# Token-major queries, softmax divided out on chip, and both signs of a head pair turned into one 128-row operand

## Chip, cores, metric

One core of a Trainium2 chip. The metric is the device time of one execution in microseconds (us). Numbers are of runs with a mean granted TensorE clock of 0.996 to 1.0, unless a text says otherwise.

## The reference

A linear-attention branch and a GELU branch over the same 2048 tokens, mixed by a gate. bf16 throughout; 16 heads of 28; the hidden layer has 1792 features.

```python
q, k, v = heads(x @ wqkv)                                  # x: [2048, 448]
pq, pk  = q @ w_phi[h], k @ w_phi[h]
phi_q   = concat(softmax(pq), softmax(-pq))                # two signs, 56 features a head
phi_k   = concat(softmax(pk), softmax(-pk))
kv, z   = phi_k^T @ v, sum over tokens of phi_k
a = (phi_q @ kv) / (phi_q . z + 1e-6), heads merged, @ wo
b = gelu(x @ w1 + b1) @ w2 + b2
g = sigmoid((x * gate_w).sum(-1))
return g * a + (1 - g) * b
```

## The kernel before

The kernel folds `w_phi` into the query and key weights (`Wpq`, `Wpk`), so that one product of x gives the scores. TensorE works through stages: start-up and first key units; query scores `pq` alternating with the last keys and values; the hidden layer `hp`, with the key-value sums `acc` in its midst; then the output stage, in which each tile of 128 tokens has numerators `nm`, the second dense product `y` over w2, and the attention output with `wo`. NPR = 8 is the number of head pairs, PW = 56, KW = 60, HP = 64, NG = 4, NK = 7, NJ = 14.

Keys are token-major: 128 tokens by all 448 features, normalised in place. Queries are feature-major and stay unnormalised; their softmax sums are carried as extra columns and divided out per tile by VectorE.

```python
def k_norm(u):                                   # keys: divide the softmax sums out
    ...
    nc.vector.reduce_sum(out=sums[:], in_=ph, axis=AX.X)
    nc.vector.reciprocal(out=rec[:], in_=sums[:])
    ...                                          # product with rec on GpSimd (unit 7: half on VectorE)

def q_pair(g, h):                                # queries: feature-major, 512 tokens wide
    pq = four("pq")
    for k in range(NK):
        for i in range(2):
            nc.tensor.matmul(pq[:, i, :], lhsT=w_half(Wpq, WqS, i, k)[:, g * P:(g + 1) * P],
                             rhs=x_half(i, k, h), ...)
    nc.scalar.activation(out=EqP[:, g, dst], in_=src, func=ACT.Exp)
    nc.scalar.activation(out=EqN[:, g, dst], in_=src, func=ACT.Exp, scale=-1.0)

def k_two(r):                                    # keys of the second half: 448 wide
    ...
            nc.tensor.matmul(pk[:, i, 0:D], lhsT=x_half(i, k, 1)[:, r * P:(r + 1) * P],
                             rhs=w_half(Wpk, WkS, i, k), ...)

def num_tile(t):
    for g in range(NG):
        for s, E in ((0, EqP), (1, EqN)):        # 8 matmuls of 120 columns
            nc.tensor.matmul(nm[s][:, g * 2 * KW:(g + 1) * 2 * KW], lhsT=E[:, g, tok],
                             rhs=KVbd[:, g, s, :], start=True, stop=True)
    ...                                          # 12 VectorE operations in all, see the diff
    nc.sync.dma_start_transpose(oT[:, :, tok], o_tok[:, t % 4, :])
```

Half of x and half of each weight are wanted on the other 64 rows, so that two 64-row matmuls can run side by side. `xS` and `WqS` are those half-swapped copies, made by transfers; `WvS` and `WkS` are made by GpSimd.

```python
swap_on_pool(WvS, WvG)                           # GpSimd copies
...
nc.gpsimd.tensor_copy(out=WkS[0:HP, 0:3, :], in_=Wpk[HP:P, 0:3, :])
nc.gpsimd.tensor_copy(out=WkS[HP:P, 0:3, :], in_=Wpk[0:HP, 0:3, :])
swap_x(0, "even")                                # transfers issued by SyncE, in this order
swap_w(WqS, Wpq)
swap_x(0, "odd")
load_x(2)
load_x(3)
swap_x(1)                                        # xS of the second half
...
for n in range(2 * NJ):                          # hidden layer, 28 units
    m_unit(n // NJ, n % NJ)
    if n == 4:
        ...                                      # key-value sums
        gates()                                  # three small VectorE operations for the gate
```

The softmax here doesn't subtract the row's maximum and nothing guards it: scores larger than these inputs give would overflow.

Of the kernel before, what the change touches and what calls it, by code (L numbers as in the profile page):

```python
# [7 lines left out]
ALU = mybir.AluOpType  # L8
ACT = mybir.ActivationFunctionType
# [3 lines left out]
S = 2048  # L13
D = 448
H = 16
DH = 28
# [19 lines left out]
def kernel(  # L36
# [42 lines left out]
    EqP = consts.tile([P, NG, S], BF16, name="EqP")  # L79
    EqN = consts.tile([P, NG, S], BF16, name="EqN")  # L80
    oT = consts.tile([P, NC4, S], BF16, name="oT")
    o_tok = consts.tile([P, 4, 512], BF16, name="o_tok")
    KVbd = consts.tile([P, NG, 2, 2 * KW], BF16, name="KVbd")
# [18 lines left out]
    Wpq = attn.tile([P, NC4, NG * P], BF16, name="Wpq")  # L102
    WqS = attn.tile([P, NC4, NG * P], BF16, name="WqS")
# [4 lines left out]
    bd = w2_sb[:, 2:6, :].rearrange("p c (h d) -> p c h d", h=H)  # L108

# [12 lines left out]
    x0 = oT[:, 0, 0:4 * D].rearrange("p (t d) -> p t d", t=4)  # L122
# [42 lines left out]
    nc.gpsimd.memset(Wpq[:].rearrange("p c (x w) -> p (c x) w", w=HP)[:, :, PW:HP], 0.0)  # L165
# [11 lines left out]
    nc.gpsimd.memset(KVbd[:], 0.0)  # L177
    for g in range(NG):
        nc.gpsimd.tensor_copy(
            out=KVbd[:, g].rearrange("p s (i w) -> p s i w", i=2)[:, :, :, KW - 2:KW],  # L180
            in_=m4[:, None, :, :].to_broadcast([P, 2, 2, 2]))
# [82 lines left out]
    def wq_at(rows, c):  # L264
        return (Wpq[rows, c, :].rearrange("p i (x w) -> p i x w", w=HP)[:, :, :, 0:PW]
                if isinstance(c, slice)
                else Wpq[rows, c, :].rearrange("p (x w) -> p x w", w=HP)[:, :, 0:PW])

    def x_half(i, k, h):
        rows = slice(i * HP, (i + 1) * HP)  # L270
        b = 2 * h + i
        if k == NK - 1:
            return xS[rows, 3, h, :] if i == 0 else xT[rows, 3, b * 512:(b + 1) * 512]
        if k % 2 == i:
            return xT[rows, k // 2, b * 512:(b + 1) * 512]
        return xS[rows, k // 2, h, :]

    def k_exp(u, pk):
        tt = slice(2 * u, 2 * u + 2)
        src = pk[:, :, 0:D].rearrange("p i (x w) -> p i x w", w=PW)  # L280
        nc.scalar.activation(out=phik[:, tt, :, 0, 0:PW], in_=src, func=ACT.Exp)  # L281
        nc.scalar.activation(out=phik[:, tt, :, 1, 0:PW], in_=src, func=ACT.Exp, scale=-1.0)  # L282

    def k_norm(u):
        tt = slice(2 * u, 2 * u + 2)
        sums = work.tile([P, 32, 2], F32, name="sums", bufs=3)
        ph = phik[:, tt].rearrange("p t x s w -> p (t x s) w")[:, :, 0:PW]
        ph = ph.rearrange("p y (h d) -> p y h d", d=DH)
        nc.vector.reduce_sum(out=sums[:], in_=ph, axis=AX.X)  # L289
        rec = work.tile([P, 32, 2], F32, name="rec", bufs=3)  # L290
        nc.vector.reciprocal(out=rec[:], in_=sums[:])  # L291
        parts = [(nc.gpsimd, 0, 32)] if u < 7 else [(nc.vector, 0, 16), (nc.gpsimd, 16, 32)]
        for eng, lo, hi in parts:
            eng.tensor_tensor(out=ph[:, lo:hi], in0=ph[:, lo:hi],  # L294
                              in1=rec[:, lo:hi, :, None].to_broadcast([P, hi - lo, 2, DH]),
                              op=ALU.mult)

# [14 lines left out]
    def w_half(W, W_S, i, k):  # L312
        rows = slice(i * HP, (i + 1) * HP)
        if k == NK - 1:
            return W_S[rows, 3, :] if i == 0 else W[rows, 3, :]
        return W[rows, k // 2, :] if k % 2 == i else W_S[rows, k // 2, :]
# [17 lines left out]
    def q_pair(g, h):  # L334
        pq = four("pq")
        for k in range(NK):
            for i in range(2):
                nc.tensor.matmul(pq[:, i, :],  # L338
                                 lhsT=w_half(Wpq, WqS, i, k)[:, g * P:(g + 1) * P],
                                 rhs=x_half(i, k, h), start=(k == 0), stop=(k == NK - 1))  # L340
        dst = slice(h * 1024, (h + 1) * 1024)
        src = pq[:].rearrange("p a b -> p (a b)")
        nc.scalar.activation(out=EqP[:, g, dst], in_=src, func=ACT.Exp)  # L343
        nc.scalar.activation(out=EqN[:, g, dst], in_=src, func=ACT.Exp, scale=-1.0)  # L344
# [9 lines left out]
    def kv_out(acc):  # L354
        src = acc[:, 0, 0:NPR * (PW + 2)].rearrange("p (g i w) -> p g i w", g=NG, i=2)
        for s in range(2):
            for i in range(2):
                rows = slice(s * HP, s * HP + PW)
                nc.vector.tensor_tensor(
                    out=KVbd[i * HP:i * HP + PW, :, s, i * KW:i * KW + PW + 2],  # L360
                    in0=src[rows, :, i, :],
                    in1=mask[rows, None, :].to_broadcast([PW, NG, PW + 2]), op=ALU.mult)
# [46 lines left out]
    x1o = oT[0:HP, 1, 0:512]  # L409
    swap_on_pool(WvS, WvG)  # L410
    x0o = oT[0:HP, 1, 512:768]
# [24 lines left out]
    nc.sync.dma_start(w2_sb[:], B_w2.rearrange("(j p) n -> p j n", p=P))  # L436
# [3 lines left out]
    for g in range(NG):  # L440
        q_pair(g, 0)
    k_norm(3)
    for r in range(4):
        k_two(r)
        v_two(r)
        k_norm(4 + r)
        q_pair(r, 1)
# [14 lines left out]
    def m_unit(h, j):  # L462
        hp = wide("hp") if h == 0 and j == 2 else pair("hp")
        for k in range(NK):
            for i in range(2):
                nc.tensor.matmul(hp[:, i, :],  # L466
                                 lhsT=w1_sb[i * HP:(i + 1) * HP, k, j * P:(j + 1) * P],
                                 rhs=x_half(i, k, h), start=(k == 0), stop=(k == NK - 1))
        if gel[h] is None:
            gel[h] = hold.tile([P, NJ, S // 2], BF16, name="gel1", tag="phik_gel")  # L470
        nc.scalar.activation(out=gel[h][:, j, :],  # L471
                             in_=hp[:].rearrange("p a b -> p (a b)"),
                             func=ACT.Gelu_apprx_tanh, bias=b1T[:, j:j + 1])

    def num_tile(t):
        tok = slice(t * P, (t + 1) * P)
        nm_ps = ps2.tile([P, 2, 512], F32, name="nm", tag="nm", bufs=2)
        nm = [nm_ps[:, 0, :], nm_ps[:, 1, :]]
        for g in range(NG):
            for s, E in ((0, EqP), (1, EqN)):  # L480
                nc.tensor.matmul(nm[s][:, g * 2 * KW:(g + 1) * 2 * KW], lhsT=E[:, g, tok],  # L481
                                 rhs=KVbd[:, g, s, :], start=True, stop=True)
        nmv = [n_[:, 0:NPR * KW].rearrange("p (x w) -> p x w", x=NPR) for n_ in nm]
        st = work.tile([P, 2, NPR, 4], F32, name="st", bufs=3)
        for s in range(2):
            nc.vector.tensor_copy(out=st[:, s], in_=nmv[s][:, :, PW:KW])  # L486
        u = work.tile([P, 2, NPR, 2], F32, name="u", bufs=3)
        nc.vector.scalar_tensor_tensor(out=u[:], in0=st[:, :, :, 2:4], scalar=5e-7,
                                       in1=st[:, :, :, 0:2], op0=ALU.mult, op1=ALU.add)
        for s in range(2):  # L490
            nc.vector.tensor_tensor(out=u[:, s], in0=u[:, s], in1=st[:, 1 - s, :, 2:4],
                                    op=ALU.mult)
        den = work.tile([P, NPR, 2], F32, name="den", bufs=3)
        nc.vector.tensor_tensor(out=den[:], in0=u[:, 0], in1=u[:, 1], op=ALU.add)
        nc.vector.reciprocal(out=den[:], in_=den[:])
        al = work.tile([P, 2, NPR, 2], F32, name="al", bufs=3)
        tmp = work.tile([P, 2, D], BF16, name="tmp", bufs=2)
        for s in range(2):
            nc.vector.scalar_tensor_tensor(out=al[:, s], in0=den[:], scalar=eL[:, t:t + 1],
                                           in1=st[:, 1 - s, :, 2:4], op0=ALU.mult, op1=ALU.mult)  # L500
        for s in range(2):
            nc.vector.tensor_tensor(  # L502
                out=tmp[:, s, :].rearrange("p (x h d) -> p x h d", x=NPR, h=2),
                in0=nmv[s][:, :, 0:PW].rearrange("p x (h d) -> p x h d", h=2),
                in1=al[:, s, :, :, None].to_broadcast([P, NPR, 2, DH]), op=ALU.mult)
        nc.vector.tensor_tensor(out=o_tok[:, t % 4, 0:D], in0=tmp[:, 0, :], in1=tmp[:, 1, :],
                                op=ALU.add)
        nc.sync.dma_start_transpose(oT[:, :, tok], o_tok[:, t % 4, :])

    for n in range(2 * NJ):  # L510
        m_unit(n // NJ, n % NJ)
        if n == 4:
            acc = wide("acc")
            for u in range(8):
                kv_sum(acc, u)
            kv_out(acc)
            gates()
# [68 lines left out]
```

## Time and profile before

| | before |
|---|---|
| time, median of 3 runs | 155.48 us (155.42 to 156.28) |
| span of the profiled run | 153.5 us |
| first query matmul | 19.72 us |
| first matmul on `xS`, in the first key group of the second half | 25.77 us |
| first hidden-layer matmul | 42.44 us |
| first numerator | 88.69 us |
| last matmul ends | 150.16 us |

The stage limits in this table come from TensorE's timeline. The busy shares and the chain of waits are shown inside the prediction. The timeline of TensorE at the start of the second half's keys (start, duration, engine, line, what, output and inputs, shape, count):

```profile
25.76 0.35 PE L330 MATMUL pk<-Wpk,xT 64*128 64x448 bf16 x1
25.77 0.54 PE L330 MATMUL pk<-WkS,xS 64*128 64x448 bf16 x2
```

The matmul on `xT` and its partner on `xS` start 0.01 us apart: nothing is waited for. That distance is the measure of a wait for `xS`. The window of the hidden layer (window, then busy time and count of TensorE, its weight loads, VectorE, ScalarE and GpSimd, then granted clock, DMA share and GB/s):

```profile
42.40:88.70 46.30, 46.30 (x523) 22.61 (x519) 5.66 (x10) 33.11 (x32) 4.20 (x2) 1.00 0.09 29
```

TensorE is busy for all of the 46.3 us, VectorE and GpSimd for some 5 us each. This is the room into which the change puts its new work.

### The profile page before, as it was taken

The numbers are of one execution on the slowest core, as the hardware profiler recorded it, in microseconds if no ns is written. First come the engines' busy times: TensorE is split into PE (matmuls) and PEld (weight loads), VectorE is DVE, ScalarE is ACT, GpSimd is POOL, SyncE is SP. The second block draws the span as 40 slices with busy tenths as digits, with TensorE's granted clock in tenths as the row PEclk, the third lists the DMA queues.
The fourth block names the chain that finished last, engine by engine and source line by source line (L and its number), as shares of the span: only waits on it lengthen the run. The fifth ranks groups of instructions, "written<-read, shape, count | busy, mean of one in ns | idle before, by whom it ended". The sixth has DMA issues, their size and how long they took to land.

```text
span 153.5 us, 3192 instructions
## 1 busy us (share of the span) xinstructions
PE 148.4 (97%) x1302; PEld 78.1 (51%) x1302; DVE 83.1 (54%) x244; ACT 77.2 (50%) x93; POOL 40.0 (26%) x43
## 2 busy tenths in 40 slices
PE   7899999999999999999999999999999999999991
PEld 2464444444444944444444455555556555555560
DVE  3442899699890050000000069999977999977100
ACT  2665989998989347777676730111311111111121
POOL 7999497979873000000000000000000000000000
PEclk9999999999999999999999999999999999999999
DMA  4997999999990000000000001133332124235401
GB/s 153 212 228 154 205 193 213 219 218 216 251 343 12 4 0 4 0 0 4 0 0 0 4 0 34 34 63 77 91 94 64 41 70 92 77 83 38 124 30 30
DMA packets 27922, 14.11 MB, mean 92 GB/s; under 512 B 19842, under 2 KB 27780, under 8 KB 27908
## 3 DMA queue, kind: packets, MB, share of 16 engines
q1 hardware_dynamic: 26692, 13.25, 39.6%
q10 hardware_dynamic: 1152, 0.65, 1.5%
q8 instruction: 10, 0.16, 0.4%
q14 instruction: 4, 0.03, 0.1%
q0 software_dynamic: 64, 0.01, 0.0%
HBM read 6.11 MB, written 1.84 MB: 52 GB/s over the span
## 4 chain that ended last, share of the span: by engine, by line
PE 91%; DMA 3%; SPq 2%; issue 0%; DVE 0%; ACT 0%; ACTq 0%
PE y L525 28%; PE hp L466 28%; PE y L531 8%; PE pq L338 8%; PE nm L481 4%; PE v_ps L322 3%; PE pk L330 3%; DMA WqT<-in_A_wqkv_dram 3%; PE pk L223 3%; PE acc L349 2%; SPq L138 2%; PE v_ps L223 2%; PE w_ps L250 1%; PE pk L226 1%; SPq L126 1%; PE v_ps L226 0%
## 5 line engine op out<-in xcount | busy, mean ns | idle before, releaser
L525 PE MATMUL y<-w_sb,gel 128*128 128x448 bf16 (+2 forms) x238 | 45.2, 342 | 0.0
L466 PE MATMUL hp<-xT,w_sb 64*128 64x512 bf16 x196 | 42.6, 376 | 0.0
L466 PE MATMUL hp<-xS,w_sb 64*128 64x512 bf16 x196 | 42.6, 376 | 0.0
L471 ACT ACTIVATE gel<-hp,b1T 128x1024 bf16<-128x1024 f32 x28 | 30.8, 1110 | 13.0 <-PE hp L466 13.0
L534 ACT ACTIVATE res<-y,ungate 128x448 bf16<-128x448 f32 (+2 forms) x17 | 10.4, 611 | 50.3 <-PE y L531 50.2
L525 PEld LDWEIGHTS <-gel 128*128 128x128 bf16 x238 | 22.6, 98 | 19.6
L466 PEld LDWEIGHTS <-w_sb 64*128 64x128 bf16 x392 | 19.0, 94 | 23.0
L294 POOL TENSOR_TENSOR phik<-phik,rec 128x1792 bf16<-128x1792 bf16 (+1 forms) x8 | 24.9, 3127 | 6.1 <-DVE rec L291 6.1
L486 DVE COPY st<-nm 128x32 f32<-128x32 f32 x32 | 4.5, 184 | 35.5 <-PE nm L481 35.5
L502 DVE TENSOR_TENSOR tmp<-nm,al 128x448 bf16<-128x448 f32 x32 | 18.4, 617 | 0.0
L289 DVE TENSOR_REDUCE sums<-phik 128x64 f32<-128x1792 bf16 x8 | 16.0, 2000 | 4.0 <-ACT phik L282 4.0
L531 PE MATMUL y<-wo_sb,oT 128*128 128x448 bf16 (+2 forms) x68 | 14.7, 341 | 0.0
L338 PE MATMUL pq<-xT,Wpq 64*128 64x512 bf16 x56 | 12.9, 376 | 0.0
L338 PE MATMUL pq<-xS,WqS 64*128 64x512 bf16 x56 | 12.9, 376 | 0.0
L343 ACT ACTIVATE EqP<-pq 128x1024 bf16<-128x1024 f32 x8 | 8.4, 1051 | 2.2 <-PE pq L338 2.2
L197 DVE CAST vaug<-v_ps 128x896 bf16<-128x896 f32 x7 | 7.5, 1081 | 2.7 <-PE v_ps L209 1.7
L281 ACT ACTIVATE phik<-pk 128x896 bf16<-128x896 f32 x8 | 7.7, 961 | 1.8 <-PE pk L228 1.8
L344 ACT ACTIVATE EqN<-pq 128x1024 bf16<-128x1024 f32 x8 | 8.4, 1055 | 0.0
L481 PE MATMUL nm<-KVbd,EqP 128*128 128x120 bf16 x64 | 8.3, 216 | 0.0
L481 PE MATMUL nm<-KVbd,EqN 128*128 128x120 bf16 x64 | 8.3, 216 | 0.0
L282 ACT ACTIVATE phik<-pk 128x896 bf16<-128x896 f32 x8 | 7.8, 972 | 0.0
L531 PEld LDWEIGHTS <-oT 128*128 128x128 bf16 x68 | 6.0, 98 | 3.5
(105 smaller groups left out, 159.8 us busy)
## 6 DMA issues: line engine op xcount, KB each, us to landing
w_sb<-in_B_w_dram SPq DMA_DIRECT2D x4, 784.0 KB, 11.6
out_dram<-res SPq DMA_DIRECT2D x15, 112.0 KB, 1.9
w_sb<-in_B_w_dram SPq DMA_DIRECT2D x1, 1568.0 KB, 16.9
xS<-xT SPq DMA_DIRECT2D x2, 256.0 KB
oT<-in_A_x_dram ACTq DMA_DIRECT2D x1, 448.0 KB, 3.1
xS<-xT SPq DMA_DIRECT2D x2, 192.0 KB, 3.6
wo_sb<-in_A_wo_dram SPq DMA_DIRECT2D x1, 336.0 KB
WqS<-Wpq SPq DMA_DIRECT2D x1, 256.0 KB, 3.2
```

Of the source, the lines that this page charges most:

```text
L289: nc.vector.reduce_sum(out=sums[:], in_=ph, axis=AX.X)
L294: eng.tensor_tensor(out=ph[:, lo:hi], in0=ph[:, lo:hi], in1=rec[:, lo:hi, :, None].to_broadcast([P, hi - lo, 2, DH]), op=ALU.mult)
L338: nc.tensor.matmul(pq[:, i, :], lhsT=w_half(Wpq, WqS, i, k)[:, g * P:(g + 1) * P], rhs=x_half(i, k, h), start=(k == 0), stop=(k == NK - 1))
L343: nc.scalar.activation(out=EqP[:, g, dst], in_=src, func=ACT.Exp)
L344: nc.scalar.activation(out=EqN[:, g, dst], in_=src, func=ACT.Exp, scale=-1.0)
L466: nc.tensor.matmul(hp[:, i, :], lhsT=w1_sb[i * HP:(i + 1) * HP, k, j * P:(j + 1) * P], rhs=x_half(i, k, h), start=(k == 0), stop=(k == NK ...
L471: nc.scalar.activation(out=gel[h][:, j, :], in_=hp[:].rearrange("p a b -> p (a b)"), func=ACT.Gelu_apprx_tanh, bias=b1T[:, j:j + 1])
L481: nc.tensor.matmul(nm[s][:, g * 2 * KW:(g + 1) * 2 * KW], lhsT=E[:, g, tok], rhs=KVbd[:, g, s, :], start=True, stop=True)
L502: nc.vector.tensor_tensor(out=tmp[:, s, :].rearrange("p (x h d) -> p x h d", x=NPR, h=2), in0=nmv[s][:, :, 0:PW].rearrange("p x (h d) -> p ...
L525: nc.tensor.matmul(y, lhsT=gel[t // 8][:, j, (t % 8) * P:(t % 8 + 1) * P], rhs=w2_sb[:, j, cols], start=(j == 0), stop=False)
L531: nc.tensor.matmul(y, lhsT=oT[:, c, tok], rhs=wo_sb[:, c, cols], start=False, stop=(c == NC4 - 1))
L534: nc.scalar.activation(out=res[:, cols], in_=y, func=ACT.Copy, scale=ungate[:, t:t + 1])
```

## The change

The intent is to give the queries the form that the keys have already: token-major scores, 448 wide, softmax sums divided out once. The normalised units are then turned by DMA into `EqT`, where the positive and negative features of a head pair fill 128 rows. A numerator then needs one 58-column matmul for a head pair instead of two 120-column ones for two pairs, and VectorE's work per tile falls from twelve operations to four. Half of the units lie in the storage of w2 until they are turned, so w2 is loaded later.

The diff, cut to its core (tile declarations, the simpler `kv_out`, weight-layout helpers and memsets are left out; the start-up's scratch for x moves from `oT` to `EqT`):

```diff
+    def q_norm(u):
+        norm(q_tok(u), 0)                        # reduce and reciprocal on VectorE, product on GpSimd
+        for i in range(2):
+            t = 8 * (u // 4) + 4 * i + u % 4
+            nc.sync.dma_start_transpose(EqT[:, :, t * P:(t + 1) * P],
+                                        q_tok(u)[:, i].rearrange("p x s w -> p (x s w)"))
...
-    def q_pair(g, h):
+    def q_two(r, h):
         pq = four("pq")
         for k in range(NK):
             for i in range(2):
-                nc.tensor.matmul(pq[:, i, :],
-                                 lhsT=w_half(Wpq, WqS, i, k)[:, g * P:(g + 1) * P],
-                                 rhs=x_half(i, k, h), start=(k == 0), stop=(k == NK - 1))
-        dst = slice(h * 1024, (h + 1) * 1024)
-        src = pq[:].rearrange("p a b -> p (a b)")
-        nc.scalar.activation(out=EqP[:, g, dst], in_=src, func=ACT.Exp)
-        nc.scalar.activation(out=EqN[:, g, dst], in_=src, func=ACT.Exp, scale=-1.0)
+                nc.tensor.matmul(pq[:, i, 0:D], lhsT=x_half(i, k, h)[:, r * P:(r + 1) * P],
+                                 rhs=w_half(Wpq, WqS, i, k), start=(k == 0), stop=(k == NK - 1))
+        two_exp(q_tok(4 * h + r), pq)
...
     v_both()
-    nc.sync.dma_start(w2_sb[:], B_w2.rearrange("(j p) n -> p j n", p=P))
     k_norm(2)
...
     def num_tile(t):
-        for g in range(NG):
-            for s, E in ((0, EqP), (1, EqN)):
-                nc.tensor.matmul(nm[s][:, g * 2 * KW:(g + 1) * 2 * KW], lhsT=E[:, g, tok],
-                                 rhs=KVbd[:, g, s, :], start=True, stop=True)
-        (two copies, six operations of 16 to 32 elements, a reciprocal,
-         two products 128x448 with al, one addition 128x448)
+        nm = ps2.tile([P, 512], F32, name="nm", tag="nm", bufs=2)
+        for x in range(NPR):
+            nc.tensor.matmul(nm[:, x * (PW + 2):(x + 1) * (PW + 2)], lhsT=EqT[:, x, tok],
+                             rhs=KV[:, x, :], start=True, stop=True)
+        (den + 1e-6, reciprocal, scale by the gate, one product 128x448)
         nc.sync.dma_start_transpose(oT[:, :, tok], o_tok[:, t % 4, :])

     for n in range(2 * NJ):
         m_unit(n // NJ, n % NJ)
+        if n < 8:
+            q_norm((0, 1, 2, 3, 4, 5, 6, 7)[n])
+        if n == 8:
+            nc.sync.dma_start(w2_sb[:], B_w2.rearrange("(j p) n -> p j n", p=P))
```

## The prediction

> **What bounds the kernel now.** I read the page's busy shares, then the chain of work that ended last, then that chain in order of time, then the timelines of single engines. The busy shares and the chain by line:
>
> ```profile
> PE 148.4 (97%) x1302; PEld 78.1 (51%) x1302; DVE 83.1 (54%) x244; ACT 77.2 (50%) x93; POOL 40.0 (26%) x43
> PE 91%; DMA 3%; SPq 2%; issue 0%; DVE 0%; ACT 0%; ACTq 0%
> PE y L525 28%; PE hp L466 28%; PE y L531 8%; PE pq L338 8%; PE nm L481 4%; PE v_ps L322 3%; PE pk L330 3%; DMA WqT<-in_A_wqkv_dram 3%; PE pk L223 3%; PE acc L349 2%; SPq L138 2%; PE v_ps L223 2%; PE w_ps L250 1%; PE pk L226 1%; SPq L126 1%; PE v_ps L226 0%
> ```
>
> The reader should see that from about 10 us to the end the chain never leaves TensorE. So time is won only by shortening TensorE's own sequence, and lost only where something makes TensorE wait. A busy figure is not throughput here, because matmuls overlap; I take costs from the start-to-start pace instead. The chain in order of time has that pace for the four stages that matter:
>
> ```profile
> 19.88 6.04 PE pq L338 x56
> 25.93 1.32 PE pk L330 x14
> ...
> 50.16 3.75 PE acc L349 x128
> ...
> 88.76 0.95 PE nm L481 x16
> 89.71 2.65 PE y L525 x14
> 92.36 0.42 PE nm L481 x8
> ```
>
> Query scores (pq): 56 matmuls, 512 columns wide, in 6.04 us, which is 1.51 us for each group of 14. Key scores (pk), the token-major form with 448 columns: 1.32 us for 14. The key-value sums (acc), 128 weight rows by 58 columns: 3.75 us / 128 = 29.3 ns each. The numerators (nm), 120 columns: 0.42 us / 8 = 52.5 ns each.
>
> [...] from 88 to 152 us its DMA records hold 8192 packets of 256 bytes for the 16 oT transposes, at 21.2 ns each; 512 packets over 16 engines are 0.68 us for 131 kB, or 193 GB/s.[...]
>
> **The change, part by part.**
>
> *Query scores.* Eight groups of 14 matmuls go from 512 columns to the shape of the pk group: 8 x (1.51 - 1.32) = 1.52 us off TensorE's path, if nothing else holds it. ScalarE's two exponentials per group go from 1024 to 896 elements, from starts 0.905 us apart to 0.80 us apart (timeline of ScalarE). It keeps pace: I followed the four rotating score buffers by hand, and each is emptied over 1 us before TensorE wants it.
>
> *A wait I expect in its place.* The first key group of the second half reads xS, the half-swapped copy of x. Here is the queue's issue of that copy, and the weight load that uses it:
>
> ```profile
> 22.74 0.59 SPq L146 DMA_DIRECT2D xS<-xT  x1
> DMA to landing us min/median/max: 2.8/2.8/2.8
> 25.55 0.31 PEld L330 LDWEIGHTS <-xS 64*128 64x128 bf16 x2
> ```
>
> Issued at 22.74 and 2.77 us in flight, it landed at 25.51; the load went at 25.55. It is just in time today. The first four query groups save 4 x 0.19 = 0.76 us, so TensorE will ask at 24.8. Only the copy of Wq is smaller (7/8 of 448 KB, perhaps 0.2 us earlier), so the landing moves to about 25.3, and I expect TensorE to wait about 0.5 us. Net of the query part: 1.52 - 0.5 = 1.0 us.
>
> *Numerators.* Both signs of a head pair are now stacked in 128 rows, so a tile has the same 8 matmuls but 58 columns instead of 120. The acc matmuls are the same shape, 128 weight rows by 58. Per tile 8 x (52.5 - 29.3) = 186 ns; 16 tiles make 2.97 us. All of it is on the path.
>
> *VectorE in the output stage.* Its work per tile falls from fifteen instructions to four. By durations now: a 16-element operation on PSUM 0.18, reciprocal 0.25, scale 0.18 and one 128x448 product 0.62, together 1.2 us against 3.1 us. TensorE's tile takes 3.8 us and waited for VectorE only once, for some 0.05 us, so this is nearly worthless.
>
> *New work in the middle.* Eight q_norm units follow the last k_norm: a reduction and a reciprocal on VectorE, 2.00 + 0.55 us, and a product on GpSimd:
>
> ```profile
> L294 POOL TENSOR_TENSOR phik<-phik,rec 128x1792 bf16<-128x1792 bf16 x7 | 22.4, 3211 | 5.1 <-DVE rec L291 5.1
> 51.00:88.70 37.70, 37.70 (x425) 18.39 (x421) 2.20 (x7) 24.80 (x23) 0.00 (x0) 1.00 0.01 2
> ```
>
> The second line is the window from 51 to 88.7 us: GpSimd 0.00, VectorE 2.20, DMA share 0.01. All three have room under the hidden layer's matmuls. GpSimd is the slowest link: it ends its key work at 47.6 us and needs 8 x 3.2 = 25.7 us, so about 73 us. Each unit is followed by two transposes of 128x1024. An oT transpose, half that size, occupies the issuing queue for:
>
> ```profile
> L508 SPq DMA_TRANSPOSE oT<-o_tok x16: 1191/1202/2066, 92.7 to 142.4; - x16
> ```
>
> The three-times-larger ones of x took 1.50 us at best, so I estimate 1.35 us per issue, 2.7 us per unit, and 2 x 1.36 us of the sixteen engines. Both are under GpSimd's 3.2 us, so the pace stays GpSimd's, and the last transpose is issued by 76 us.
>
> *The load of w2 moves behind them.* Its storage holds the query units of the second half. Issued at about 76.5 us instead of:
>
> ```profile
> 30.74 0.46 SPq L436 DMA_DIRECT2D w_sb<-in_B_w_dram  x1
> w_sb<-in_B_w_dram SPq DMA_DIRECT2D x1, 1568.0 KB, 16.9
> ```
>
> The 16.9 us are mostly queueing behind w1. The trace moves w2's 896-byte packets at some 420 per us once alone, so 1792 packets take 4.3 us, plus about 2 us to start: landed near 83 us. TensorE needs it when the first dense product starts, 89.7 us now and about 88.3 after. Some 5 us spare, so it costs nothing.
>
> *The sum.* 155.48 - 1.0 - 2.97 = 151.5 us, a ratio of 0.974.
>
> **Rivals.**
>
> *w2 late.* If a transpose takes 2 us or more of the issuing queue, or GpSimd is slower beside VectorE and DMA, the chain of eight ends past 82 us, w2 lands past 88, and each further microsecond is a wait of TensorE. At 2.4 us per transpose the queue needs 8 x 4.8 us after about 51 us, ends near 90, and w2 lands near 96: the gain is gone and the time is 157 to 159. For it: transposes of x took up to 2.26 us to issue. Against it: those had other transfers in the queue, and the undisturbed oT ones took 1.20. I give it one chance in ten.
>
> *No wait for xS.* If the smaller Wq copy, or a shift of the queue, brings xS earlier, the query part saves its full 1.52 us: 151.0. If the wait is the full 0.75 us, 151.7. Both stay near the centre.
>
> *Small matmuls not at 29 ns.* The acc stage is one run of 128; here only 8 stand between wide ones, and each numerator set now waits for two transfers' flags as well. If switching costs 0.1 us per tile, 1.6 us of the 2.97 are lost: 153.1, within 2%. Against it: the present tiles of 8 show exactly 8 x 52.5 ns, no switching cost. One in seven.
>
> *VectorE or ScalarE become the bound.* I see nothing for it: VectorE's added 20 us lie where it is idle, and the last score buffers are emptied sooner than now.
>
> **Range and chances.** The faster verdict needs 152.4 or less. The centre 151.5 leaves 0.9 us for switching costs and the xS wait together. With the late-w2 case and the switching case I put 0.72 on faster, 0.23 on within 2%, 0.05 on slower. Range 150.6 to 153.0.
>
> **What would show it.** In the changed profile: query groups at 1.32 us in the chain; a gap on TensorE of 0.3 to 0.7 us near 25 us put down to DMA xS; nm x8 at about 0.24 us per tile; GpSimd busy until about 73 us; w2 landing near 83 us with no wait before the first dense product. I am wrong if TensorE waits for w2 before about 89 us, if nm stays above 0.35 us per tile, or if a new wait stands in the hidden layer's stage.

(It counts fifteen VectorE instructions per tile before; the code has twelve. The 3.1 us that it uses came from their durations in the trace, and nothing rested on the count. That matmuls overlap shows in its trace by the numerators: 216 ns each, started 52.5 ns apart. Its 2 us for a load to start are an estimate; the nearest figure of the trace is the transpose of `oT`, 2.4 us from issue to landing with 0.68 us of packets.)

## The result

The changed kernel takes 151.14 us, median of 4 runs (150.36 to 151.81), against 155.60 us for the kernel before in the same rounds (155.42 to 156.28, 4 runs). The ratio is 0.970, 95% interval 0.964 to 0.976: faster. Ratios here are the mean time of one kernel's fast runs over that of the other's of the same rounds, so not quite the ratio of the medians quoted. All outputs are right.

The profiled run of the changed kernel happens to be its slowest of four (151.81 us). TensorE's stages in it, beside those of before:

| stage, by the first matmul of each | before us | after us | difference |
|---|---|---|---|
| start to first query matmul | 19.72 | 20.00 | +0.28 |
| queries, keys, values of the second half | 22.72 | 22.38 | -0.34 |
| hidden layer with key-value sums | 46.25 | 46.43 | +0.18 |
| output stage, to the last matmul's end | 61.47 | 58.34 | -3.13 |
| last matmul's end to the end of the span | 3.34 | 2.96 | -0.38 |
| span | 153.50 | 150.11 | -3.39 |

Almost all the gain of this pair lies in the output stage. The query stage gave 0.34 us although its groups became shorter as intended. Even of this, 0.18 us only moved to the next row. In the changed kernel's profile the matmul on `xT` runs one step ahead of its partner from the wait on, so the first hidden-layer matmul starts 0.18 us before its partner; in the kernel before the two start together. From the first query matmul to the first numerator, which is free of this shift, it is 68.97 us before and 68.81 after: a gain of 0.16 us. The chain in order of time shows both (start, duration, what):

```profile
14.24 2.25 SPq L153
...
19.43 4.36 DMA xT<-in_A_x_dram
23.81 2.77 DMA xS<-xT
26.63 1.50 PE pk L343 x13
...
29.46 1.32 PE pq L351 x14
...
88.89 0.56 PE nm L483 x16
89.45 2.65 PE y L518 x14
92.09 0.23 PE nm L483 x8
```

A query group (`pq`) takes 1.32 us, as foreseen, and a tile's numerators 0.23 us where they took 0.42. But the chain no longer runs through TensorE alone: before 26.6 us it leads back through `xS`, then the load of x that `xS` is copied from, then the issuing queue. TensorE's timeline at that place has the wait:

```profile
25.30 0.35 PE L343 MATMUL pk<-Wpk,xT 64*128 64x448 bf16 x1
26.63 0.36 PE L343 MATMUL pk<-WkS,xS 64*128 64x448 bf16 x2 [0.98 <-DMA xS<-xT]
```

The bracket is the idle time and its releaser. The two matmuls that started 0.01 us apart before now start 1.33 us apart. This is the wait that the prediction put at 0.5 us.

The middle has the new work. The window of the hidden layer, columns as before:

```profile
42.40:88.70 46.30, 46.30 (x523) 23.67 (x519) 29.36 (x25) 32.90 (x32) 30.14 (x10) 1.00 0.68 129
```

VectorE went from 5.66 to 29.36 us and GpSimd from 4.20 to 30.14, DMA from a share of 0.09 to 0.68, and TensorE is still busy for the whole 46.30. So the new work is hidden. How narrowly, GpSimd's timeline and then the issuing queue's show:

```profile
48.98 12.72 POOL L297 TENSOR_TENSOR oT<-oT,rec 128x1792 bf16<-128x1792 bf16 x4 [1.11 <-DVE rec L294]
61.66 3.21 POOL L297 TENSOR_TENSOR w_sb<-w_sb,rec 128x1792 bf16<-128x1792 bf16 x1
67.80 6.38 POOL L297 TENSOR_TENSOR w_sb<-w_sb,rec 128x1792 bf16<-128x1792 bf16 x2 [2.93 <-DVE rec L294]
74.14 3.21 POOL L297 TENSOR_TENSOR phq<-phq,rec 128x1792 bf16<-128x1792 bf16 x1
```

```profile
77.38 2.60 SPq L308 DMA_TRANSPOSE EqT<-phq  x2
80.21 0.41 SPq L504 DMA_DIRECT2D w_sb<-in_B_w_dram  x1
```

The products begin at 48.98 us instead of the 47.6 foreseen and have a gap of 2.93 us in the middle, so GpSimd ends at 77.4 us instead of 73. The load of w2 (`w_sb` here) is issued at 80.21 instead of 76.5 and takes 7.6 us, landing at 87.83. The first dense product starts at 89.28. Of the 5 us of slack, 1.4 us are left.

What made the gap is in VectorE's timeline. Two of the three gate operations of the diff's context stand ahead of the next unit's sums. After:

```profile
59.48 2.25 DVE L457 TENSOR_SCALAR eL<-eL 128x16 f32<-128x16 f32 x1
61.76 3.14 DVE L458 TENSOR_SCALAR ungate<-eL 128x16 f32<-128x16 f32 x1
```

and the same two in the kernel before, where no GpSimd product runs beside them:

```profile
55.62 0.17 DVE L453 TENSOR_SCALAR eL<-eL 128x16 f32<-128x16 f32 x1
55.83 0.18 DVE L454 TENSOR_SCALAR ungate<-eL 128x16 f32<-128x16 f32 x1
```

An operation of sixteen elements a row took 3.14 us instead of 0.18. The first ended at 61.73, when the group of four GpSimd products did (48.98 + 12.72 = 61.70), the second at 64.90, when the next product did (61.66 + 3.21 = 64.87). So each ended within 0.03 us of the end of a GpSimd product; by what mechanism was not shown. The reductions and reciprocals beside the same products were not held up (1.96 to 1.99 and 0.55 us each, against 2.00 and 0.55 in the kernel before).

### The profile page after: what moved, and what is told of

It reads as the page before. It is cut to its first block, busy times and chain, and to the rows that moved or that the text cites. A ratio compares the mean times of both kernels' runs of the same rounds, so it can differ in the third digit from the quotient of the medians.

```text
span 150.1 us, 3123 instructions
## 1 busy us (share of the span) xinstructions
PE 145.1 (97%) x1302; PEld 77.3 (51%) x1302; DVE 79.7 (53%) x129; ACT 75.7 (50%) x93; POOL 65.7 (44%) x48
## 4 chain that ended last, share of the span: by engine, by line
PE 87%; DMA 5%; SPq 4%; DVE 1%; issue 0%; ACT 0%; ACTq 0%
PE hp L470 28%; PE y L518 28%; PE y L524 8%; PE pk L343 4%; PE v_ps L335 4%; PE pq L351 4%; DMA xT<-in_A_x_dram 3%; PE nm L483 2%; PE acc L358 2%; PE v_ps L212 2%; PE warm_ps L389 2%; DMA xS<-xT 2%; SPq L153 2%; PE w_ps L253 1%; PE xp L372 1%; SPq L140 1%
## 5 line engine op out<-in xcount | busy, mean ns | idle before, releaser
L470 PE MATMUL hp<-xS,w_sb 64*128 64x512 bf16 x196 | 42.1, 376 | 0.0
L470 PEld LDWEIGHTS <-w_sb 64*128 64x128 bf16 x392 | 20.1, 94 | 22.0
L487 DVE TENSOR_SCALAR den<-nm 128x16 f32<-128x16 f32 x16 | 2.8, 173 | 42.7 <-PE nm L483 42.7
L297 POOL TENSOR_TENSOR oT<-oT,rec 128x1792 bf16<-128x1792 bf16 x4 | 12.7, 3211 | 1.1 <-DVE rec L294 1.1
L351 PE MATMUL pq<-Wpq,xT 64*128 64x448 bf16 x56 | 11.8, 349 | 0.0
L297 POOL TENSOR_TENSOR w_sb<-w_sb,rec 128x1792 bf16<-128x1792 bf16 x3 | 9.6, 3212 | 2.9 <-DVE rec L294 2.9
L351 PE MATMUL pq<-WqS,xS 64*128 64x448 bf16 x56 | 10.5, 349 | 0.0
L493 DVE TENSOR_TENSOR o_tok<-nm,al 128x448 bf16<-128x448 f32 x16 | 10.0, 625 | 0.6
L294 DVE RECIPROCAL rec<-sums 128x64 f32<-128x64 f32 x16 | 8.8, 553 | 1.4
L292 DVE TENSOR_REDUCE sums<-oT 128x64 f32<-128x1792 bf16 x4 | 7.9, 1982 | 0.0
```

What stands on the lines that cost most here:

```text
L297: eng.tensor_tensor(out=ph[:, lo:hi], in0=ph[:, lo:hi], in1=rec[:, lo:hi, :, None].to_broadcast([P, hi - lo, 2, DH]), op=ALU.mult)
L351: nc.tensor.matmul(pq[:, i, 0:D], lhsT=x_half(i, k, h)[:, r * P:(r + 1) * P], rhs=w_half(Wpq, WqS, i, k), start=(k == 0), stop=(k == NK - 1))
L470: nc.tensor.matmul(hp[:, i, :], lhsT=w1_sb[i * HP:(i + 1) * HP, k, j * P:(j + 1) * P], rhs=x_half(i, k, h), start=(k == 0), stop=(k == NK ...
L493: nc.vector.tensor_tensor(out=o_tok[:, t % 4, 0:D].rearrange("p (x h d) -> p x h d", x=NPR, h=2), in0=nmv[:, :, 0:PW].rearrange("p x (h d) ...
```

## Experiments

The theory after this reading: (1) the output stage's gain is the fewer columns of the numerators; (2) the query stage's gain is real and partly eaten by the wait for `xS`; (3) the middle work is hidden, with w2's slack the narrow point. The main rival to (1) was that VectorE's lighter work is what shortened the stage, and to (2) that the query groups would not have shortened the time in any case.

Experiments were run in three sets, each beside its own runs of the kernel before (medians 155.32, 155.30 and 155.34 us). The unaltered changed kernel (after_again) was run in the first set only, so where nm_wide and the runs below it in the table are compared with it, the comparison crosses sets; the ratios are the safer measure there. All kernels are the changed one with the edit shown, except the control, which edits the kernel before.

| run | edit | median us (range, n) | ratio to before [95%] |
|---|---|---|---|
| after_again | none | 150.46 (150.28 to 150.71, 4) | 0.9689 [0.9676, 0.9701] |
| wq_on_act | copy of Wq issued by ScalarE | 151.39 (150.78 to 151.82, 5) | 0.9745 [0.9725, 0.9765] |
| gates_late | gate operations later | 150.45 (150.2 to 151.3, 5) | 0.9693 [0.967, 0.9715] |
| both | the last two together | 151.22 (150.97 to 153.23, 5) | 0.9768 [0.9728, 0.9808] |
| nm_wide | numerators 120 columns again | 153.55 (153.39 to 153.75, 4) | 0.9882 [0.9868, 0.9896] |
| dve_long | 7 idle VectorE operations per tile | 152.23 (151.62 to 152.52, 5) | 0.9778 [0.9757, 0.9799] |
| q_wide | query matmuls 512 columns again | 151.77 (151.5 to 152.12, 4) | 0.9768 [0.975, 0.9785] |
| wq_on_pool | copy of Wq made by GpSimd | 150.13 (149.94 to 150.23, 4) | 0.9659 [0.9646, 0.9673] |
| dve_as_before | VectorE's sequence as long as before | 151.31 (150.53 to 151.48, 5) | 0.9727 [0.9708, 0.9746] |
| w2_later | w2 held back by idle GpSimd work | 155.31 (153.74 to 156.02, 5) | 0.9988 [0.9948, 1.0027] |
| before_wq_on_pool | kernel before, copy of Wq by GpSimd | 155.89 (155.73 to 155.9, 5) | 1.0033 [1.0021, 1.0045] |
| pool_and_gates | wq_on_pool and gates_late | 150.27 (150.13 to 150.38, 4) | 0.9673 [0.9661, 0.9686] |

### after_again: the changed kernel once more

No edit.

> The changed kernel unaltered, as the base of this set. Both theories: 150.4 to 151.8 us, a ratio near 0.970. What is to be learned is how steady two places of the first profile are: TensorE's wait for xS near 25 us (1.33 us between the first two key matmuls there, of which 0.2 us is the ordinary pace) and the landing of w2 (87.8 us, first dense product at 89.5). If the wait for xS is a chance of one run it should change by over 0.5 us here.

Measured: 150.46 us; the wait for `xS` is smaller in this profile, 0.52 us from start to start:

```profile
24.85 0.35 PE L343 MATMUL pk<-Wpk,xT 64*128 64x448 bf16 x1
25.37 0.36 PE L343 MATMUL pk<-WkS,xS 64*128 64x448 bf16 x2 [0.18 <-DMA xS<-xT]
```

What differs upstream is one issue of SyncE's queue, the small copy at L153 (first fence the changed kernel's first profile, second this run's):

```profile
14.24 2.25 SPq L153 DMA_DIRECT2D xS<-xT  x1
16.54 1.55 SPq L140 DMA_TRANSPOSE xT<-in_A_x_dram  x1
```

```profile
13.78 0.62 SPq L153 DMA_DIRECT2D xS<-xT  x1
14.46 2.25 SPq L140 DMA_TRANSPOSE xT<-in_A_x_dram  x1
```

In one execution the small copy's issue took 2.25 us, in the other 0.62 and the next one took 2.25. Over the seven profiles whose start-up is the changed kernel's (the first, this one, gates_late, nm_wide, dve_long, dve_as_before, w2_later) the start-to-start wait was 1.33, 0.52, 0.98, 0.64, 0.92, 0.86 and 0.43 us, mean 0.81. So the wait is there each time, and its size is a matter of the execution. It would also account for the changed kernel's larger scatter in the first rounds.

### wq_on_act: is it SyncE's issuing time that delays xS?

```diff
     def swap_w(W_S, W):
-        nc.sync.dma_start(W_S[0:HP, :, :], W[HP:P, :, :])
-        nc.sync.dma_start(W_S[HP:P, 0:3, :], W[0:HP, 0:3, :])
+        nc.scalar.dma_start(W_S[0:HP, :, :], W[HP:P, :, :])
+        nc.scalar.dma_start(W_S[HP:P, 0:3, :], W[0:HP, 0:3, :])
```

> The two swapped copies of Wq are issued by ScalarE's queue instead of SyncE's; nothing else changes. My theory: the query part gained nothing net because xS landed at 26.6 us behind a blocked SyncE queue. With two issues (1.1 us) gone from in front of it, SyncE is ahead by 1 to 2.7 us, xS lands before 25.3, TensorE's wait near 25 us vanishes, and the kernel gains 0.8 to 1.3 us on the unaltered one of this set. Risk inside the theory: WqS then shares the DMA engines with the loads of x and may land later than 20 us, which would give some of it back at the first query group. Rival A: the transfers are bound by the sixteen engines, not by the issue, so xS lands as late as before and the time is the same within 0.3 us. Rival B: TensorE gains 1.2 us but meets w2 (landed 1.6 us before it was needed), so the gain is capped.

Measured: 151.39 us, slower than after_again. The wait for `xS` has gone (25.47 and 25.59 us), but another has come in its place. The chain:

```profile
14.22 6.04 DMA WqS<-Wpq
20.30 5.45 PE pq L351 x55
25.75 1.32 PE pk L343 x14
```

Now the first query group waits for the copy of Wq, 6 us in flight, while the other start-up transfers are under way. The theory in this form falls: freeing issue slots of SyncE moved the wait to another transfer. The profiled run (150.78) is the fastest of the five, and in it the exchange is about even: the query groups lose 0.42 us to the new wait, and from the first query matmul to the first numerator it takes 67.90 us against 68.02 in after_again. That the slower runs waited longer for the copy of Wq is likely (in the run `both`, two further on, TensorE waits 2.77 us for it), and not shown here. This suggests that the transfer engines themselves are short in that stretch, which was argued here and not measured by itself.

### gates_late: does the GpSimd gap cost time?

```diff
             kv_out(acc)
+        if n == 8:
             gates()
```

> The three small VectorE operations for the gate move from behind the key-value sums to behind the last query unit. In the profile two of them took 2.25 and 3.14 us instead of 0.18, each ending where a GpSimd product ended, and GpSimd then sat idle 2.9 us for its next reciprocal. Theory: with them moved, that idle goes, GpSimd ends about 74.4 instead of 77.4 us, w2 lands near 85 instead of 87.8, and the time is the same within 0.3 us, because w2 was early enough by 1.6 us. Rival: w2 is on the path in some unprofiled runs; then the median falls by 0.5 us or more and the scatter shrinks.

Measured: 150.45 us against 150.46, no difference, as expected. GpSimd's gap is gone:

```profile
60.81 9.55 POOL L297 TENSOR_TENSOR w_sb<-w_sb,rec 128x1792 bf16<-128x1792 bf16 x3
70.32 3.21 POOL L297 TENSOR_TENSOR phq<-phq,rec 128x1792 bf16<-128x1792 bf16 x1
```

GpSimd ends at 73.5, which is the predicted 73; w2 is issued at 77.37 (76.5 predicted) and lands at 84.72 instead of 86.92. From GpSimd's first product on query scores to its last end it takes 25.4 us, against 28.4 in both profiles of the unaltered changed kernel. So the gate operations explain most of the late issue (77.37 is still 0.9 us past the 76.5), the flight of 7.35 us most of the rest, and the time shows that the slack was enough either way.

### both: the two edits together

The diffs of the last two.

> Both edits at once. Theory: the gain of the first edit alone, 0.8 to 1.3 us, and no more: about 149.9 us. Rival B above (w2 caps the gain of the first edit): then this one is faster than the first edit alone by up to 1 us, since it takes the cap away.

Measured: 151.22 us, with one fast run at 153.23 (and a slow one, at a clock of 0.986, left out); the verdict on faster by 2% is unclear. The profile is of the run at 153.23. The chain again shows the copy of Wq, this time with a flight of over 8 us, and TensorE standing still until 22.7 us:

```profile
14.41 8.28 DMA WqS<-Wpq
22.73 5.45 PE pq L351 x55
```

Moving the copy of Wq to ScalarE's queue is a bad trade here too; the combination teaches nothing on the gates.

### nm_wide: are the columns the output stage's gain?

```diff
-            nc.tensor.matmul(nm[:, x * (PW + 2):(x + 1) * (PW + 2)], lhsT=EqT[:, x, tok],
-                             rhs=KV[:, x, :], start=True, stop=True)
+            lo, n_col = x * (PW + 2), min(2 * KW, 512 - x * (PW + 2))
+            nc.tensor.matmul(nm[:, lo:lo + n_col], lhsT=EqT[:, x, tok],
+                             rhs=KV[:].rearrange("p x w -> p (x w)")[:, lo:lo + n_col],
+                             start=True, stop=True, skip_group_check=True)
```

Each matmul is as wide as before (the last, 106 columns, is cut at the buffer's end) and writes over the next pair's place, which that pair's own matmul then overwrites. VectorE's four operations stay. KV is padded with two pairs of zeros.

> The numerator matmuls stream 120 columns again (106 for the last of each tile), the extra ones being overwritten by the next; the stacked operand, the short VectorE sequence and everything else stay. Theory: the gain of the numerator part is TensorE's columns alone, so a tile goes from 0.23 back to 0.42 us and the kernel loses 16 x 0.18 = 2.9 us on the changed kernel (150.5 in the set before): about 153.4. Rival: the gain came from the shorter VectorE sequence behind each tile; then nothing changes, within 0.3 us.

Measured: 153.55 us, 3.1 us more than after_again. The chain has the 16 numerators and the 8 of one tile at nearly the duration of before:

```profile
87.83 0.93 PE nm L485 x16
...
91.42 0.41 PE nm L485 x8
```

The output stage takes 61.33 us where after_again's takes 58.34. The gain of that stage is TensorE's columns; with them restored and VectorE still light, it is gone.

### dve_long: is VectorE's lighter work worth anything?

```diff
         nmv = nm[:, 0:NPR * (PW + 2)].rearrange("p (x w) -> p x w", x=NPR)
+        (two copies 128x32, three operations 128x16 to 128x32, two products 128x448 into a
+         scratch tile; nothing uses their results)
         den = work.tile([P, NPR, 2], F32, name="den", bufs=3)
```

> Seven idle VectorE operations per output tile are put back (two copies, one scale-and-add, two small products, two 128x448 products; 2.1 us by their durations before), results unused; TensorE is untouched. VectorE then takes about 3.3 us per tile against TensorE's 3.64. Theory: same time as the changed kernel within 0.3 us, since VectorE is off the path. Rival: the shorter VectorE sequence was worth something: slower by 1 us or more, up to 3.

Measured: 152.23 us, 1.8 us more than after_again and against the theory, which expected next to nothing. The output stage grew by 1.24 us (59.58 against 58.34). Part of it lies in one place of the chain:

```profile
114.29 0.24 PE nm L483 x8
...
115.46 1.69 DMA out_dram<-res
117.16 0.61 DVE o_tok L508
117.79 4.31 DMA oT<-o_tok
122.15 0.93 PE y L539 x4
```

Here TensorE waits for a tile of `oT` whose way led over VectorE's last product and a transposing transfer of 4.31 us. The profile also puts a wait of 0.5 us of a numerator down to VectorE's last product, which holds the nm buffer. In this version that product comes last and reads the buffer for all of VectorE's 3 us, which the kernel before did not do: there the last operation works on copies. (The nm buffer is one of the kernel's PSUM tiles, which its matmuls write to.) So dve_long is a harsher case than the kernel before, and a fairer one was needed.

### dve_as_before: VectorE's sequence of before, in its own order

The same added operations, but the two products come after `al` and make the result, and the last operation is a maximum of the two equal products, outside PSUM, so that the nm buffer comes free earlier.

```diff
-        nc.vector.tensor_tensor(out=o_tok ..., in0=nmv ..., in1=al ..., op=ALU.mult)
+        for s in range(2):
+            nc.vector.tensor_tensor(out=tmp[:, s, :] ..., in0=nmv ..., in1=al ..., op=ALU.mult)
+        nc.vector.tensor_tensor(out=o_tok[:, t % 4, 0:D], in0=tmp[:, 0, :], in1=tmp[:, 1, :],
+                                op=ALU.max)
```

> A fairer form of the long VectorE sequence, after the first one cost 1.7 us against my theory: the extra operations stand in the order of the kernel before, with the last read of PSUM 0.4 us ahead of the end and the output tile written by a last 448-element operation; about 3.0 us per tile, results correct. Theory now: with TensorE at 3.64 us per tile, VectorE at 3.0 is not a throughput bound, but each tile's output reaches its transpose 1.8 us later, and TensorE waits where two numerator sets follow each other; I expect 0.3 to 1.2 us over the changed kernel (150.5). Rival A: free, as predicted (within 0.3 us); then the 1.7 us of the first form came from its late PSUM release alone. Rival B: 1.5 us or more again; then the shorter VectorE sequence carries about half of the numerator gain.

Measured: 151.31 us by the median, 0.8 us over after_again's set. By stages only 0.22 us of it belong to VectorE: the output stage takes 58.56 us against 58.34. It is visible in the third and fourth tile, and gone after:

```profile
91.55 0.34 PE nm L483 x8
...
94.53 0.34 PE nm L483 x8
...
98.27 0.23 PE nm L483 x8
```

In that profile the start was 0.37 us later than in after_again's and the wait for `xS` 0.34 us longer. So VectorE's share is about 0.2 us of the gain by this profile; the rest of the median's difference is the start-up's scatter as far as one profile can tell. (The intervals of the two ratios do not overlap, so that rest is argued and not shown; the unaltered kernel itself had a median of 151.14 us in one round and 150.46 in another.)

### q_wide: is the query stage's gain real?

```diff
-    Wpq = attn.tile([P, NC4, D], BF16, name="Wpq")
-    WqS = attn.tile([P, NC4, D], BF16, name="WqS")
+    Wpq = attn.tile([P, NC4, 512], BF16, name="Wpq")      # the last 64 columns zero
+    WqS = attn.tile([P, NC4, 512], BF16, name="WqS")
...
-                nc.tensor.matmul(pq[:, i, 0:D], lhsT=x_half(i, k, h)[:, r * P:(r + 1) * P],
+                nc.tensor.matmul(pq[:, i, :], lhsT=x_half(i, k, h)[:, r * P:(r + 1) * P],
```

> The token-major query matmuls stream 512 columns again (64 of zeros), and with them the copy of Wq regains its old size; the rest stays. Gross, 8 groups x 0.19 = 1.52 us come back. Theory: part of that was never won, because TensorE waited 0.5 to 1.3 us for xS at the first key group (three profiles: 1.33, 0.52, 0.98); with the wider groups it arrives later and the wait shrinks to nearly nothing, so the loss on the changed kernel is 0.4 to 1.0 us. Rival: the wait has another cause and stays; then the loss is the full 1.5 us.

Measured: 151.77 us, 1.3 us more than after_again. The query stage is back at 22.72 us, exactly that of before, against after_again's 21.58, and the wait for `xS` is gone (25.70 and 25.71):

```profile
19.82 6.04 PE pq L352 x56
25.87 1.32 PE pk L344 x14
```

From the first query matmul to the first numerator it takes 68.98 us, again that of before (68.97), against 68.02 in after_again; the stage's own difference, 1.14, holds the shift of 0.18 us told above. So the narrower queries are worth 0.96 us net by these profiles and 1.3 by the medians. The profiles lie inside what the theory expected, the medians between it and its rival. The run shows also that the wait is a consequence of the shorter groups: TensorE asks for `xS` earlier than before.

### wq_on_pool: the copy of Wq without a transfer

```diff
+    swap_on_pool(WqS, Wpq)
     swap_x(0, "even")
-    swap_w(WqS, Wpq)
     swap_x(0, "odd")
```

> The swapped copies of Wq are made by GpSimd, which sat idle 16.5 to 18.7 us, and not by DMA at all: 392 KB and two issues leave the queue that the loads of x stand in. Moving their issue to ScalarE had removed the wait for xS but made WqS itself late (first query group waited up to 2.4 us), so the sixteen engines, not the issue, are short in this stretch. Theory: with the bytes gone, xS lands 1 to 2 us earlier, before 24.8, the wait disappears, and the kernel gains 0.5 to 1.0 us on the changed one (150.5): about 149.8. Risk: two copies of 3.0 us in all end near 19.6 us, and the first query group may wait a few tenths; the first key product on GpSimd starts some 0.9 us later, which its later idle time absorbs. Rival: no gain, because w2 or the next transfer takes the place of the wait.

Measured: 150.13 us, the fastest of all. The wait has vanished:

```profile
24.91 0.35 PE L343 MATMUL pk<-Wpk,xT 64*128 64x448 bf16 x1
24.91 0.54 PE L343 MATMUL pk<-WkS,xS 64*128 64x448 bf16 x2
```

`xS` landed at 23.57 us, and the query stage took 21.23 us, which is 1.49 less than before and nearly the full 8 x 0.19 = 1.52. Here the stretch from the first query matmul to the first numerator takes 67.48 us, and in each of the seven profiles with a wait it takes 67.48 us plus the start-to-start wait, within 0.02 us (68.81 with 1.33, 68.02 with 0.52, 67.91 with 0.43). So the wait for `xS` is all that the query part lost. The edit takes bytes and two issues out of the queue at once and does not tell which of the two counted. The gain over after_again is 0.3 us by the medians and 0.5 by the ratios, at or under the low end of what was expected, and the scatter fell from 0.43 to 0.29 us.

### before_wq_on_pool: the control

The same edit in the kernel before.

> The control for the GpSimd copies of Wq: the same edit in the kernel before. There xS landed at 25.51 and was asked for at 25.55, just in time. Theory: no wait to remove, so 155.3 within 0.3 us. Rival: the edit gains by itself (less DMA traffic early), 0.4 us or more, and then its gain in the changed kernel says nothing of the wait for xS.

Measured: 155.89 us, 0.5 us slower than the kernel before, which neither the theory (within 0.3 us) nor its rival (a gain) expected. Its query stage is 22.72 us as without the edit; in the profiles it is the first query matmul that comes 0.41 us later (20.13 against 19.72), and the end after the last matmul takes 0.11 us more. So the edit is no general improvement: it helped the kernel in which TensorE asks for `xS` too early, and not the one in which it does not.

### pool_and_gates: both good edits

> GpSimd copies of Wq together with the late gate operations, the candidate for the best version. Theory: no wait for xS, and w2 landing near 84 us, far from the path: 150.1 us as with the copies alone, within 0.3. If w2 had been in the way in some runs of that one, this one is faster by more than 0.3 us or scatters less.

Measured: 150.27 us. w2 lands at 83.44 us instead of wq_on_pool's 86.06, which is 2.6 us more slack, and it is worth nothing here. Intervals of the two overlap.

### w2_later: what if the slack runs out?

```diff
             q_norm((0, 1, 2, 3, 4, 5, 6, 7)[n])
+        if n == 6:
+            pad = work.tile([P, 2048], BF16, name="pad", bufs=1)
+            for _ in range(2):
+                nc.gpsimd.tensor_copy(out=pad[:], in_=phq3[:] ...)     # 3.85 us in all
```

> Two idle GpSimd copies of 128x2048, about 1.9 us each, stand before the last query units, so the load of w2 is issued some 3.8 us later. In the profiles of the changed kernel w2 landed at 86.9 and 87.8 us, and the first dense product started at 88.2 and 89.5. Theory: the spare time is 1.5 us, not the 5 us I predicted; TensorE now waits for w2 before the first dense product and the kernel loses 3.8 - 1.5 = 2.3 us (152.8). Rival: the load goes faster or the dense products do not all need it at once, and the time stays at 150.5.

Measured: 155.31 us (five fast runs), 4.9 us more than after_again: the whole gain is gone for 3.85 us of GpSimd work that nobody reads. w2 was issued at 83.04 instead of 79.47 and landed at 91.48 instead of 86.92. The timeline and, below it, the window of the slow stretch (columns as before) show where it went:

```profile
91.62 4.49 PE L522 MATMUL y<-w_sb,gel 128*128 128x448 bf16 x14 [3.26 <-DMA w_sb<-in_B_w_dram]
```

```profile
92.08:95.49 3.41, 3.41 (x11) 1.37 (x10) 0.00 (x0) 0.00 (x0) 0.00 (x0) 0.50 0.19 38
```

TensorE stood still for 3.26 us, and soon after the granted clock was 0.50 for 3.41 us; the first dense product took 4.49 us where the same view of after_again has 2.81. Counted from the first numerator, the dense product began 3.41 us later than in after_again (3.88 against 0.47), and the slow clock added 4.49 - 2.81 = 1.68. Together that is 5.09 us, and the output stage took 63.44 us instead of 58.34, which is 5.10. The theory expected a loss of 2.3 us: it had the wait too short and no price for the clock. The six runs give a cross-check. Five had a mean clock of 0.987 to 0.989 (one of them counted as slow), which is what one such stretch makes (half of 3.41 us in 154 is 0.011). The sixth kept 1.0 and took 153.74 us, 3.3 us over after_again, about as much as the wait alone.

In this trace the last numerator before the wait starts at 88.17 us and the next matmul at 91.62, 3.45 us without a start, and from 92.08 to 95.49 the granted clock is 0.50. By the mean clocks that happened in five executions (0.987 to 0.989) and not in the sixth (1.0); what decides it was not shown.

The landing came 4.56 us later than in after_again (3.57 from the issue, 0.99 from a longer flight) and the first dense product 3.59 us later, so 1.0 us of slack took up the rest. That agrees with the slack read from landing and use: 1.4 us in the first profile, 88.03 - 86.92 = 1.1 in after_again.

## Why the prediction was right, and where not

*TensorE is the path and the output stage gains by its columns: right.* 2.97 us foreseen; 3.13 by the stages, and 3.0 by stages when nm_wide put the columns back (3.1 by the medians).

*No switching cost of short runs of small matmuls: right.* The rival would have made it 0.33 us per tile; the chain has 0.23, so 29 ns for each matmul, the pace of the key-value sums.

*Query groups at 1.32 us, and a wait for `xS` in place of part of the gain: right in kind, the term 0.5 us mis-sized.* It was 0.43 to 1.33 us, mean 0.81, over seven profiles. The landing was predicted at 25.3; it was 26.6 in the first profile and 25.3 in after_again, where the wait was the predicted one. What the estimate lacked is the scatter of issue durations on the queue: in both profiles one issue takes 2.25 us, but not the same one. Net of the wait, the prediction's 1.0 us compares with 0.16 us in the first profile and 0.96 in the second (from the first query matmul to the first numerator). wq_on_pool, beside its control, shows that the wait is what takes the difference: without it the gain is 1.49 us.

*The middle work is hidden: right.* TensorE is busy for all 46.30 us of that window in both kernels.

*GpSimd done at 73 us, w2 with 5 us to spare: wrong, without a cost.* GpSimd ended at 77.4 and 1.4 us were left. That the time came out right all the same is owed to the size of the margin, and not to this part of the estimate. Three terms were off. The first product began 1.4 us later. GpSimd's pace was held to be its own, while the gate operations on VectorE, held up beside GpSimd's products (2.25 and 3.14 us instead of 0.17 and 0.18), delayed the next sums and left GpSimd idle for 2.93 us; gates_late removes just that and gets 73.5. And the flight of w2 was 7.6 us instead of 6.3, which was a figure from packets alone on the engines. The rival "w2 late" was given one chance in ten on account of the transposes' issue time. Those took 1.2 to 1.3 us as estimated; the way that came near was another. And w2_later shows that the rival's price was too low: the prediction counted each microsecond past the need as a wait, and beyond the wait there was the clock, 0.50 for 3.41 us in that profile, so that a start 3.4 us late cost 5.1.

*VectorE's lighter work is nearly worthless: right at the size, for a narrower reason than given.* The estimate reasoned with the tile time of before. With TensorE faster, the old sequence would cost about 0.2 us (dve_as_before), and one that holds the nm buffer longer 1.2 us (dve_long).

*Not foreseen:* the last matmul's end to the end of the span, 0.38 us less. It was about 2.95 us in most versions of the changed kernel and 3.1 in the two with the copy of Wq on GpSimd. The traces of the first pair are alike up to 2.79 us after the last matmul; then GpSimd's last closing semaphore instruction comes at 3.23 us in the kernel before and at 2.85 in the changed one. So the difference lies in the program's closing steps; why GpSimd is later there, no experiment looked at, and it stays open.

The sum was 3.97 us foreseen, 4.5 measured in the first rounds and 4.9 in after_again's. The excess over the foreseen sum is of the size of the unforeseen tail (0.4) and the output stage's extra 0.2, though the scatter from run to run is as large.

## What to carry to other kernels

In a stage that TensorE bounds, count columns of each matmul and take the pace from a stage in the same kernel with the same shape: that gave the largest term within 6%. When a stage becomes shorter, look next at what was only just in time before (here a copy that landed 0.04 us ahead of its use), and note that giving a transfer to another queue may only move the wait, as here to a copy of Wq 6.04 us in flight (wq_on_act), while making that copy on GpSimd removed it (wq_on_pool, the pair's starts both at 24.91 us). A load that moves behind a chain of work needs its slack measured, not only estimated: the chain was lengthened here by operations that have nothing to do with it (GpSimd idle for 2.93 us behind two gate operations), and the late weight of w2_later cost, beside its wait of 3.26 us, a stretch of 3.41 us at a granted clock of 0.50.

## What else the traces show

- Transposing transfers: 256-byte packets on sixteen engines took 21.2 ns (`oT` in the kernel before) and 24.6 ns (`EqT` in the changed kernel's first profile), which is 193 and 166 GB/s, and while the queries were turned no slice of that page shows more than 194 GB/s. One transpose of 128x1024 took 3.1 to 4.8 us from issue to landing, 3.7 in the median.
- Small matmuls: those of 120 columns, each with its own weight load, ran at 52.5 ns in runs of 8, and those of 58 columns at 29 ns in runs of 8 as in the run of 128.
- Small VectorE operations beside GpSimd products: two of 128x16 fp32 elements took 2.25 and 3.14 us instead of 0.17 and 0.18, each until a GpSimd product ended.
- Issues on SyncE's queue: one that took 0.6 us in one execution took 2.25 in another. In the profiles of the first pair such a long issue coincided with a 16 KB record on the instruction queue (in the changed kernel the issue at 14.24 lasted 2.25 us, the record at 14.22 some 1.9; in the kernel before the issue at 14.72 lasted 2.26, the record at 15.54 some 1.0). It is an association in two profiles, not a tested cause.
